# A new issue order and new PSUM banks for an attention and gated feed-forward kernel

## The chip, the cores and the metric

The kernel runs on one core of a Trainium2 chip. Its time is the device time of one launch in microseconds (us); lower is better. Each matmul's inputs are bf16, the tensors in memory are float32.

## The reference

For each of 8 batches and 8 heads (sequence 1024, head size 64) K and V are projected along the sequence to 64 rows, the queries attend to those 64 rows, and the heads are joined to rows of 512. Each of the 8192 rows then goes through a gated layer: 512 to 1536 twice (gate and value), the product of both, and 1536 back to 512.

```python
def _attn_ref(q, k, v, E, F):
    k_proj = np.einsum('ks,bhsd->bhkd', E, k)
    v_proj = np.einsum('ks,bhsd->bhkd', F, v)
    scores = 1.0 / np.sqrt(q.shape[-1]) * np.matmul(q, k_proj.transpose(0, 1, 3, 2))
    scores = scores - np.max(scores, axis=-1, keepdims=True)
    attn = np.exp(scores)
    attn = attn / (np.sum(attn, axis=-1, keepdims=True) + 1e-09)
    return np.matmul(attn, v_proj)

def _moe_ref(x, w_gate, w_val, w_out):
    gate = 1.0 / (1.0 + np.exp(-(x @ w_gate)))
    return gate * (x @ w_val) @ w_out

x = attn_out.transpose(0, 2, 1, 3).reshape(8192, 512)   # between the two
```

## The kernel before

**Stages.** For each batch, K and V (tiles KVs) are loaded by GpSimd's DMA queue in two halves each (KV00 and KV01 for K, KV10 and KV11 for V; 4 heads in each), and Q (tile Qb) in two halves, Q0 and Q1. TensorE projects K and V with E and F (tile EFT) in one job, `kv` (L1494, 16 matmuls). ScalarE keeps the result in kpd, and SyncE turns it with a transposing DMA into kpD (L1523). SyncE also turns Q with four transposing DMAs, qT0 to qT3 (`transpose_q`, L1480); qT0 and qT1 need Q0, qT2 and qT3 need Q1. Scores, exponentials and sums follow, SyncE turns the exponentials (eT, four DMAs), TensorE multiplies them by V, and SyncE turns the joined rows into xT (four DMAs). The gated layer on a block of 512 rows uses sums of blocks of its operands (xS, tG, tV, hS), so that a product of 2 x 2 blocks takes seven block products and not eight (`quad_jobs`, `seven`, `o_jobs`). The output leaves in stores on SyncE's queue, 256 KB each.

Batch p + 2 is loaded, and batch p + 1 attended to, while the rows of batch p go through the gated layer. The first batch is apart: it is loaded in smaller pieces, in step with the weights (wG, wV), and K, Q and the exponentials are turned on TensorE, which at the start waits for loads anyway. There 35 fills, matmuls of an identity that nobody reads (`busy`, L720, 128x256, into a bank of their own), stand between the useful ones.

**Order.** The program is cut into 2902 jobs, each for one engine (some matmuls into one bank, one copy, one DMA issue). ORDER is a written-out list of their numbers, with -1 for a fill, and PLACES names the PSUM bank, or the number of the working buffer, of each of 906 slots. Nothing else decides: `Scheduler.job` takes a time `release` for each job and makes no use of it, and `Scheduler.run` only reads the two lists.

```python
    def job(self, eng, pos, body, release=0.0, name=""):
        self.jobs.append(Job(eng, body, name))
...
        for s, p in zip(slots, PLACES):
            s.at = p
        return [fill if i < 0 else self.jobs[i].body for i in ORDER]
```

Each engine runs its own jobs in the order of the list, and waits by semaphores for what they read, or for readers of what they overwrite; a DMA issue waits in its engine's line like any other instruction. TensorE's fills and SyncE's and GpSimd's DMA issues all stand in this one list.

The times in K_AT, Q_AT, V_AT (L784) and LAND (L1011), when loads are taken to land, are used for `release` alone.

**Names in the profile.** pA and pF are PSUM banks; all matmuls are recorded at L518, ScalarE's copies at L532, GpSimd's DMA issues at L559, the transposing DMAs at L1483 (qT), L1526 (kpD) and L1741 (xT), and the stores at L1302.

Of the kernel before, what the change touches and what calls it, by code (L numbers as in the profile page):

```python
# [153 lines left out]
class Job:  # L154
# [5 lines left out]
    0, -1, -1, -1, 1, 2, -1, -1, -1, -1, -1, -1, 14, 3, -1, 4, 15, 12, 5, -1, 6, 13, -1, 16, 22, 17, -1, 7, 23,  # L160
    18, 19, 8, -1, -1, -1, 24, 34, 9, 20, 25, -1, -1, 10, 32, 35, 11, 21, 33, 26, -1, -1, -1, -1, -1, -1, -1,
    -1, -1, 36, 42, 28, 37, 52, 43, 38, 53, 39, 27, 44, 54, 29, -1, 30, 45, 40, 59, 55, 31, 46, -1, -1, -1, -1,
    -1, 56, 41, 60, 57, 47, 48, 58, 169, 61, -1, -1, 50, 49, 119, 62, 168, 51, 112, 346, 63, 118, 174, 64, 65,
    113, 124, 176, 128, 126, 125, 180, 130, 129, 127, 178, 114, 131, 115, 116, 165, 120, 68, 175, 122, 66, 121,
    69, 67, 123, 86, 88, 179, 87, 76, 70, 89, 136, 71, 177, 77, 144, 72, 140, 181, 78, 73, 90, 79, 74, 96, 167,
    152, 146, 164, 91, 142, 148, 154, 97, 75, 138, 153, 92, 132, 93, 155, 94, 149, 134, 80, 145, 98, 160, 81,
    147, 99, 161, 95, 117, 150, 162, 151, 82, 133, 100, 84, 83, 102, 101, 85, 137, 103, 190, 166, 106, 135, 104,
    108, 183, 141, 163, 107, 139, 105, 301, 187, 192, 109, 185, 302, 143, 198, 110, 214, 111, 199, 182, 278,
    170, 215, 262, 189, 303, 200, 171, 263, 216, 184, 191, 202, 201, 173, 264, 304, 188, 266, 203, 172, 217,
    218, 305, 205, 279, 196, 230, 193, 219, 186, 204, 265, 395, 280, 206, 221, 281, 267, 220, 222, 209, 207,  # L170
    269, 223, 210, 246, 270, 396, 211, 231, 225, 212, 227, 234, 197, 247, 308, 232, 397, 208, 273, 233, 250,
    226, 309, 248, 235, 398, 236, 251, 237, 213, 228, 253, 274, 224, 294, 238, 229, 254, 239, 252, 295, 241,
    249, 296, 243, 307, 255, 240, 282, 297, 257, 244, 242, 259, 256, 306, 537, 298, 258, 283, 299, 245, 260,
    285, 531, 156, 286, 261, 300, 538, 535, 289, 158, 533, 157, 290, 323, 159, 332, 314, 310, 315, 337, 319,
    429, 311, 194, 312, 316, 313, 324, 317, 426, 320, 430, 318, 333, 325, 334, 326, 328, 321, 427, 423, 329,
    322, 428, 338, 335, 327, 330, 339, 331, 268, 431, 195, 424, 341, 336, 347, 271, 354, 340, 284, 355, 351,
    342, 356, 432, 425, 352, 357, 348, 343, 349, 272, 287, 350, 344, 353, 288, 345, 359, 366, 433, 363, 275,
    367, 532, 539, 291, 434, 534, 368, 549, 360, 358, 276, 361, 369, 546, 364, 362, 365, 375, 547, 292, 378,
    370, 376, 371, 536, 548, 550, 372, 377, 277, 551, 379, 373, 293, 380, 383, 390, 374, 552, 391, 384, 385,
    540, 381, 392, 553, 541, 386, 382, 387, 555, 545, 388, 393, 389, 556, 415, 394, 499, 416, 515, 417, 500,  # L180
    418, 435, 516, 501, 436, 503, 542, 502, 519, 517, 504, 439, 520, 518, 437, 440, 522, 557, 505, 438, 400,
    521, 523, 451, 402, 506, 524, 442, 507, 401, 526, 443, 508, 510, 544, 441, 554, 511, 512, 543, 446, 452,
    513, 528, 447, 444, 453, 399, 455, 419, 445, 448, 529, 456, 483, 421, 514, 558, 527, 509, 467, 420, 484,
    454, 559, 422, 530, 458, 468, 487, 449, 403, 459, 489, 560, 488, 471, 404, 525, 462, 564, 472, 490, 463,
    457, 491, 766, 474, 473, 768, 475, 460, 485, 469, 476, 669, 470, 494, 486, 480, 670, 478, 450, 492, 464,
    479, 770, 671, 481, 477, 685, 461, 409, 482, 493, 672, 686, 495, 406, 765, 673, 410, 675, 465, 405, 674,
    496, 769, 689, 411, 676, 466, 690, 412, 771, 497, 677, 687, 413, 678, 733, 407, 688, 692, 414, 682, 498,
    679, 749, 408, 693, 767, 691, 734, 680, 683, 696, 563, 681, 694, 735, 561, 750, 772, 695, 736, 751, 697,
    773, 565, 737, 752, 684, 774, 738, 566, 583, 753, 567, 740, 584, 569, 568, 775, 570, 754, 578, 741, 777,
    585, 780, 779, 571, 744, 574, 579, 781, 572, 575, 586, 756, 573, 745, 698, 580, 782, 592, 576, 587, 701,  # L190
    581, 562, 588, 785, 577, 593, 757, 596, 582, 786, 702, 589, 760, 597, 787, 705, 590, 594, 703, 789, 591,
    598, 704, 601, 761, 595, 790, 599, 602, 699, 605, 608, 603, 707, 600, 606, 706, 609, 717, 700, 604, 610,
    739, 607, 791, 617, 611, 708, 742, 718, 613, 755, 709, 778, 614, 612, 618, 719, 615, 619, 721, 743, 758,
    616, 746, 722, 720, 620, 712, 621, 625, 759, 783, 622, 713, 626, 623, 710, 784, 747, 776, 724, 711, 624,
    762, 788, 627, 629, 748, 637, 628, 714, 630, 638, 796, 725, 631, 641, 792, 639, 715, 728, 640, 642, 763,
    716, 632, 644, 905, 633, 645, 643, 646, 906, 634, 900, 764, 723, 635, 793, 726, 647, 636, 867, 729, 803,
    868, 665, 883, 648, 902, 804, 730, 667, 869, 666, 731, 805, 668, 870, 871, 794, 806, 807, 727, 872, 809,
    797, 808, 795, 819, 732, 798, 874, 907, 899, 810, 875, 908, 904, 811, 901, 878, 652, 812, 873, 879, 814,
    649, 903, 816, 884, 876, 651, 914, 815, 813, 887, 820, 880, 885, 877, 881, 821, 888, 817, 823, 835, 799,
    824, 909, 886, 836, 822, 890, 912, 826, 801, 891, 851, 839, 650, 889, 840, 910, 894, 892, 882, 837, 895,  # L200
    915, 911, 838, 842, 827, 896, 852, 653, 917, 843, 897, 855, 913, 893, 853, 856, 830, 854, 858, 831, 841,
    859, 846, 800, 857, 898, 802, 847, 862, 860, 916, 825, 918, 654, 828, 659, 863, 844, 845, 656, 864, 861,
    660, 1037, 829, 919, 655, 1038, 848, 661, 1039, 849, 920, 663, 1133, 1040, 832, 865, 1053, 921, 657, 1041,
    833, 1054, 923, 1137, 818, 662, 1057, 850, 1135, 1055, 1042, 922, 924, 1058, 658, 834, 1044, 1060, 1134,
    1045, 1056, 926, 664, 866, 1043, 925, 927, 1138, 1061, 1046, 1101, 928, 1059, 1102, 1117, 1062, 932, 1047,
    933, 1050, 931, 934, 929, 1105, 1051, 1103, 1048, 1063, 1104, 1066, 1049, 935, 937, 1064, 1136, 936, 1139,
    1067, 1118, 1140, 1065, 1119, 938, 1141, 1121, 1120, 1106, 946, 1142, 1122, 939, 942, 947, 1124, 940, 1143,
    943, 1052, 941, 1125, 1108, 948, 1145, 1147, 951, 944, 1148, 1109, 952, 955, 1146, 945, 1112, 956, 949,
    1149, 1113, 953, 1144, 950, 960, 1150, 1069, 957, 964, 954, 1153, 961, 930, 1070, 1154, 962, 958, 1071, 965,
    963, 959, 969, 1073, 970, 1155, 966, 1128, 971, 1123, 1068, 967, 1157, 972, 1129, 1072, 968, 973, 1085,  # L210
    1074, 974, 976, 981, 1076, 977, 982, 978, 975, 1158, 1086, 1126, 979, 983, 988, 985, 1087, 1077, 986, 980,
    989, 984, 1130, 987, 990, 993, 1088, 997, 1089, 991, 994, 1107, 998, 1131, 1090, 1075, 992, 995, 1110, 1080,
    1159, 1092, 999, 1111, 1000, 1078, 1114, 1093, 1009, 1001, 1151, 1115, 1081, 1002, 1152, 1010, 1127, 1116,
    1003, 1005, 1011, 1091, 1006, 1012, 1156, 1096, 996, 1007, 1082, 1079, 1097, 1163, 1273, 1008, 1004, 1083,
    1274, 1013, 1033, 1014, 1235, 1132, 1164, 1015, 1160, 1236, 1034, 1171, 1016, 1094, 1237, 1172, 1161, 1238,
    1095, 1187, 1162, 1275, 1173, 1084, 1268, 1239, 1166, 1035, 1098, 1174, 1165, 1272, 1175, 1240, 1270, 1251,
    1267, 1188, 1242, 1176, 1269, 1189, 1243, 1178, 1022, 1099, 1191, 1179, 1282, 1036, 1100, 1192, 1182, 1190,
    1252, 1246, 1019, 1271, 1183, 1194, 1247, 1167, 1020, 1241, 1195, 1255, 1244, 1018, 1193, 1256, 1169, 1198,
    1017, 1253, 1199, 1258, 1177, 1259, 1248, 1180, 1262, 1026, 1254, 1203, 1276, 1196, 1204, 1025, 1184, 1263,
    1181, 1205, 1197, 1257, 1206, 1283, 1249, 1219, 1260, 1284, 1277, 1185, 1220, 1200, 1245, 1278, 1207, 1201,  # L220
# [155 lines left out]
def bass_linformer_attn__then__ffn_glu_sigmoid_kernel(  # L376
# [20 lines left out]
    with contextlib.ExitStack() as es:  # L397
# [383 lines left out]


        def first_batch():
            K_AT, Q_AT = ((6.4, 8.05), (10.65, 12.0)), ((9.35, 13.4), (28.8, 30.1))  # L784
            V_AT = ((15.9, 15.9), (18.35, 19.45))
            ENGS = ("ACT", "DVE", "POOL")

# [1117 lines left out]
```

## Time and profile before

| | |
|---|---|
| time, median of 3 runs | 518.26 us (517.63 to 518.54) |
| the profiled execution | 518.57 us, its span 516.8 us |
| clock of TensorE granted | 1.00 in every slice |
| TensorE busy | 510.5 us, 99% of the span, 4741 matmuls |
| VectorE, ScalarE, GpSimd busy | 436.6, 374.4, 169.8 us |
| moved by DMA | 71.57 MB, 138 GB/s in the mean |
| hardware queue (SyncE's), software queue (GpSimd's) | 40.91 MB in 104560 packets, 29.89 MB in 35904 |

The span is the time from the first to the last instruction of the profiled execution; the launch takes 1.8 us more. The profile models the end of a matmul, so that a busy TensorE may still hold small gaps: from start to start a fill of 256 columns takes 0.109 us, while its row shows 0.274. Shares are of the span, and "x" is a number of instructions. A transposing DMA is issued by SyncE (SPq), and its landing is later than the end of its issue.

### The profile page before, as it was taken

Reading aid. Unit: us, or ns where it says so; the run is one execution under the profiler, and the core shown is the slowest. Engines: PE = TensorE matmul, PEld = TensorE weight load, DVE = VectorE, ACT = ScalarE, POOL = GpSimd, SP = SyncE. Lnnn points to the kernel's source line nnn. Section 1 sums busy time; section 2 is a strip of 40 time slices with the busy share of each in tenths; the row PEclk is TensorE's granted clock in tenths of the full one; section 3 lists DMA queues with packets and bytes.
Section 4 is the critical chain, followed back from the end, with each engine's and each line's share of the span. In section 5 each row is a group of like instructions: output and inputs, shape, how many; then the busy total and the mean of one; then the engine's idle time right before and its main releaser. Section 6 shows DMA issues by size and latency. Waiting matters only on the chain.

```text
span 516.8 us, 12171 instructions
## 1 busy us (share of the span) xinstructions
PE 510.5 (99%) x4741; PEld 426.6 (83%) x4741; DVE 436.6 (84%) x849; ACT 374.4 (72%) x714; POOL 169.8 (33%) x196
## 2 busy tenths in 40 slices
PE   8999999999999999999999999999999999999997
PEld 4555867889988899888998888888998889988884
DVE  6769998699988899869997799978989889968771
ACT  1566956888876796767867789777878679686652
POOL 9882004520435033340245113620053502403020
PEclk9999999999999999999999999999999999999999
DMA  9999938896679946995579957796545994530204
GB/s 159 198 198 207 181 70 175 136 201 124 148 148 170 188 92 128 155 179 115 119 143 174 158 103 128 156 196 113 142 98 129 202 169 104 96 90 1 82 2 162
DMA packets 140521, 71.57 MB, mean 138 GB/s; under 512 B 97200, under 2 KB 132272, under 8 KB 140464
## 3 DMA queue, kind: packets, MB, share of 16 engines
q1 hardware_dynamic: 104560, 40.91, 37.8%
q0 software_dynamic: 35904, 29.89, 37.8%
q8 instruction: 37, 0.61, 0.5%
q14 instruction: 20, 0.16, 0.1%
HBM read 60.29 MB, written 16.78 MB: 149 GB/s over the span
## 4 chain that ended last, share of the span: by engine, by line
PE 55%; DMA 3%; issue 1%; POOL 1%; ACT 0%; POOLq 0%
PE pF L518 28%; PE pA L518 27%; DMA KVs<-in_k_dram 3%; POOL KVs L559 0%; POOL Qb L559 0%; ACT ost L532 0%; POOL xS L547 0%; POOLq L129 0%
## 5 line engine op out<-in xcount | busy, mean ns | idle before, releaser
L532 ACT ACTIVATE spare<-pF 128x512 f32<-128x512 f32 (+2 forms) x167 | 94.2, 574 | 32.0 <-PE pF L518 22.7
L547 POOL TENSOR_TENSOR hT<-hT,hS 128x512 bf16<-128x512 bf16 x42 | 48.1, 1164 | 174.2 <-PE pA L518 96.8
L532 ACT ACTIVATE spare<-pA 128x512 f32<-128x512 f32 (+2 forms) x146 | 83.7, 586 | 20.2 <-PE pA L518 16.3
L1724 POOL TENSOR_TENSOR KVs<-spare,inv 128x384 bf16<-128x384 f32 (+1 forms) x41 | 29.6, 731 | 84.4 <-DVE topf L1635 35.3
L532 ACT ACTIVATE spare<-spare 128x512 f32<-128x512 f32 x74 | 46.1, 628 | 5.9 <-DVE spare L1146 5.5
L1146 DVE TENSOR_TENSOR spare<-pF,spare 128x512 f32<-128x512 f32 x59 | 40.1, 681 | 10.5 <-PE pF L518 5.2
L1215 DVE SCALAR_TENSOR_TENSOR hT<-spare,pF 128x512 bf16<-128x512 f32 x60 | 40.8, 679 | 7.7 <-PE pF L518 3.7
L518 PE MATMUL pA<-wO,hT 128*128 128x256 bf16 (+1 forms) x336 | 47.2, 280 | 0.0
L1146 DVE TENSOR_TENSOR spare<-pA,spare 128x512 f32<-128x512 f32 x54 | 36.7, 681 | 8.8 <-PE pA L518 6.4
L1215 DVE SCALAR_TENSOR_TENSOR hT<-spare,pA 128x512 bf16<-128x512 f32 x52 | 35.3, 678 | 8.3 <-PE pF L518 4.1
L518 PE MATMUL pF<-wO,hT 128*128 128x256 bf16 (+1 forms) x276 | 42.2, 296 | 0.0
L518 PE MATMUL pF<-xT,wV 128*128 128x256 bf16 (+1 forms) x248 | 39.9, 283 | 0.0
L518 PEld LDWEIGHTS pA<-wO,hT 128*128 128x128 bf16 x336 | 32.8, 98 | 6.5 <-ACT KVs L532 0.2
L518 PE MATMUL pA<-xS,wV 128*128 128x256 bf16 x248 | 37.2, 273 | 0.0
L518 PE MATMUL pA<-xT,wG 128*128 128x256 bf16 (+1 forms) x220 | 35.4, 284 | 0.6 <-DVE xT L876 0.5
L518 PE MATMUL pF<-xS,wG 128*128 128x256 bf16 x232 | 34.1, 272 | 0.0
L518 PEld LDWEIGHTS pF<-wO,hT 128*128 128x128 bf16 x276 | 26.6, 98 | 8.7
L518 PE MATMUL pF<-xS,tV 128*128 128x256 bf16 x224 | 33.6, 273 | 0.0
L518 PE MATMUL pA<-xS,tG 128*128 128x256 bf16 x208 | 31.2, 273 | 0.0
L518 PE MATMUL pF<-xT,wG 128*128 128x256 bf16 (+1 forms) x188 | 30.9, 286 | 0.0
L532 ACT ACTIVATE EF<-pA 128x512 f32<-128x512 f32 (+2 forms) x35 | 19.7, 564 | 14.4 <-PE pA L518 13.5
L518 PEld LDWEIGHTS pF<-xT,wV 128*128 128x128 bf16 x248 | 23.9, 98 | 4.3
(186 smaller groups left out, 1288.7 us busy)
## 6 DMA issues: line engine op xcount, KB each, us to landing
out_dram<-ost SPq DMA_DIRECT2D x63, 256.0 KB, 2.4
KVs<-in_v_dram POOLq DMA_DIRECT2D x15, 512.0 KB, 9.4
KVs<-in_k_dram POOLq DMA_DIRECT2D x14, 512.0 KB, 10.2
Qb<-in_q_dram POOLq DMA_DIRECT2D x14, 512.0 KB, 8.8
wO<-in_moe_w_out_dram POOLq DMA_DIRECT2D x1, 1536.0 KB, 28.1
wG<-in_moe_w_gate_dram POOLq DMA_DIRECT2D x5, 256.0 KB, 16.9
wV<-in_moe_w_val_dram POOLq DMA_DIRECT2D x5, 256.0 KB, 17.3
KVs<-in_k_dram POOLq DMA_DIRECT2D x4, 256.0 KB, 6.8
```

Source lines behind the costliest of these rows:

```text
L518: lambda e: e.matmul(o, lhsT, rhs, **kw),
L532: lambda e: e.activation(o, i, func, scale=scale),
L547: fn = lambda e: e.tensor_tensor(o, a, b, op)
L1146: lambda e: e.tensor_tensor(PB(b)[:, :] if stay else BF(s), PB(b)[:, :], BF(s), ALU.add),
L1215: lambda e: e.scalar_tensor_tensor(o, y.rearrange("p (j c) -> p j c", j=2), 1.0, x.rearrange("p (j c) -> p j c", j=2), ALU.add, ALU.mult,),
L1724: fn = lambda e: e.tensor_tensor(xto.rearrange("p (g h d) -> p h g d", g=2, h=H)[:, hh[0] : hh[1], :, :], o[:, :, 0:DH].rearrange("p (h g) ...
```

## The change

ORDER is another permutation of the same 2902 jobs, with 58 fills where there were 35; the 23 more stand, as all the fills, in the first part of the list (the last one is entry 123, it was entry 94). PLACES holds other numbers in its 906 entries. The times of K_AT, Q_AT, V_AT and LAND are new too. So TensorE has 4764 matmuls instead of 4741; all other engines have as many instructions as before, in another order, and the DMAs move the same bytes.

The first 25 loads of GpSimd's queue keep their order. Later the order within each batch's six loads is another one, and so is the order of SyncE's transposes and stores. In batch 4, of which the prediction speaks, jobs 1017 to 1022 are the loads KV00, KV01, KV10, KV11, Q0 and Q1, jobs 1023 to 1026 the transposes qT0 to qT3, and job 1027 is `kv`. The order before was 1022, 1019, 1020, 1018, 1017, 1026, 1025, 1021, 1027, 1024, 1023; it becomes 1018, 1017, 1021, 1022, 1019, 1020, 1025, 1023, 1026, 1027, 1024.

From issue to use, counted in TensorE time along the list, the shortest stretches are 3.6, 4.2 and 4.3 us for kpD in batches 3, 4 and 5 (the shortest was 5.1) and 3.9 us for eT in batches 4 and 5 (it was 4.9).

The diff, cut to its core:

```diff
 ORDER = (
-    0, -1, -1, -1, 1, 2, -1, -1, -1, -1, -1, -1, 14, 3, -1, 4, 15, 12, 5, -1, 6, 13, -1, 16, 22, 17, -1, 7, 23,
-    18, 19, 8, -1, -1, -1, 24, 34, 9, 20, 25, -1, -1, 10, 32, 35, 11, 21, 33, 26, -1, -1, -1, -1, -1, -1, -1,
-    -1, -1, 36, 42, 28, 37, 52, 43, 38, 53, 39, 27, 44, 54, 29, -1, 30, 45, 40, 59, 55, 31, 46, -1, -1, -1, -1,
-    -1, 56, 41, 60, 57, 47, 48, 58, 169, 61, -1, -1, 50, 49, 119, 62, 168, 51, 112, 346, 63, 118, 174, 64, 65,
...
+    0, -1, -1, -1, -1, -1, -1, 1, 2, 3, -1, -1, -1, -1, -1, -1, -1, 14, 12, 15, 4, 13, 5, -1, -1, -1, -1, -1, 6,
+    22, 16, 23, -1, -1, -1, 7, 17, 24, 8, 25, -1, -1, -1, -1, 32, 9, 34, 26, 33, -1, 10, 18, 11, 35, 19, 27, -1,
+    -1, -1, -1, -1, 42, 36, 43, -1, 30, 31, 37, -1, -1, -1, 44, 52, 45, 20, 53, 38, 21, 54, 55, 46, -1, -1, -1,
+    -1, -1, -1, 28, 39, 59, 168, 29, 40, -1, -1, -1, -1, 56, 60, 57, 47, 58, 169, 41, 61, -1, -1, -1, -1, -1,
+    -1, -1, -1, -1, -1, 48, 50, 62, 49, 113, 51, -1, -1, -1, 63, 174, 112, 64, 65, 119, 118, 346, 128, 165, 125,
...
 PLACES = (
-    0, 2, 4, 1, 3, 1, 5, 0, 6, 1, 0, 2, 2, 0, 3, 2, 4, 3, 2, 0, 1, 0, 1, 5, 5, 0, 5, 0, 4, 8, 5, 9, 0, 1, 7, 0,
...
+    0, 3, 4, 2, 2, 1, 6, 1, 5, 0, 2, 0, 0, 1, 4, 3, 3, 2, 1, 2, 1, 1, 2, 0, 0, 1, 7, 0, 1, 7, 7, 9, 5, 7, 0, 7,
...
-            K_AT, Q_AT = ((6.4, 8.05), (10.65, 12.0)), ((9.35, 13.4), (28.8, 30.1))
-            V_AT = ((15.9, 15.9), (18.35, 19.45))
+            K_AT, Q_AT = ((7.05, 8.4), (11.1, 12.45)), ((9.8, 13.75), (29.1, 30.45))
+            V_AT = ((16.35, 16.35), (17.7, 20.3))
...
         LAND = {
-            "G": (20.1, 21.45, 26.1, 34.2, 23.5, 31.5, 36.85),
-            "V": (20.75, 22.15, 27.5, 35.5, 24.8, 32.9, 38.25),
+            "G": (20.5, 21.75, 26.4, 34.65, 23.75, 32.1, 37.3),
+            "V": (21.05, 22.45, 27.8, 36.0, 25.05, 33.35, 38.7),
         }
```

## The prediction

> **What bounds the kernel now.** I read the page first (busy shares, then the chain of waits), then TensorE's waits, the windows of the start, and around the one wait left the chain, SyncE's timeline and the landings of single transfers.
>
> ```profile
> PE 510.5 (99%) x4741; PEld 426.6 (83%) x4741; DVE 436.6 (84%) x849; ACT 374.4 (72%) x714; POOL 169.8 (33%) x196
> PE 55%; DMA 3%; issue 1%; POOL 1%; ACT 0%; POOLq 0%
> PE pF L518 28%; PE pA L518 27%; DMA KVs<-in_k_dram 3%; POOL KVs L559 0%; POOL Qb L559 0%; ACT ost L532 0%; POOL xS L547 0%; POOLq L129 0%
> ```
>
> TensorE is busy for 99% of the span, and the chain holds little but its matmuls and one load of K. An order that does the same matmuls can gain only where TensorE waits. All of its waits (total us, times, longest):
>
> ```profile
> PE pA L518 <- DMA KVs<-in_k_dram: 1.1, 2, 0.9
> PE pA L518 <- DVE tV L642: 1.1, 1, 1.1
> PE pA L518 <- DVE xT L876: 0.5, 1, 0.5
> PE pF L518 <- ACT EFT L532: 0.3, 1, 0.3
> PE pF L518 <- ACT eT L532: 0.2, 1, 0.2
> PE pF L518 <- ACT kpd L532: 0.2, 1, 0.2
> ```
>
> The same list from 50 us on keeps only the 0.9 us on K. Everything else is in the start (window; PE, PEld, DVE, ACT, POOL busy; clock; DMA share; GB/s):
>
> ```profile
> 5.00:10.00 5.00, 4.60 (x38) 3.06 (x37) 2.99 (x10) 0.60 (x1) 5.00 (x8) 1.00 1.36 175
> 10.00:15.00 5.00, 4.57 (x59) 3.15 (x57) 3.64 (x10) 1.49 (x3) 5.00 (x8) 1.00 1.38 201
> 20.00:25.00 5.00, 4.79 (x47) 2.11 (x46) 3.46 (x8) 2.61 (x5) 3.13 (x4) 1.00 1.45 195
> 45.00:50.00 5.00, 4.47 (x50) 3.03 (x48) 5.00 (x13) 3.92 (x9) 0.07 (x1) 1.00 1.24 208
> 50.00:60.00 10.00, 10.00 (x94) 8.70 (x92) 10.00 (x20) 9.10 (x19) 0.00 (x0) 1.00 1.24 207
> ```
>
> Up to 50 us the loads run at about 200 GB/s and TensorE has small holes; some of its work there is fills, which compute nothing:
>
> ```profile
> L518 PE MATMUL pA<-ident 128*128 128x256 bf16 x35 | 5.8, 274 | 0.0
> ```
>
> (274 ns includes a modelled end; from start to start a fill takes 0.109 us, so 35 take 3.8 us.) The late wait, as the chain shows it (start, us):
>
> ```profile
> 212.36 2.25 POOL KVs L559 x3
> 214.61 16.57 DMA KVs<-in_k_dram
> 231.17 0.04 issue
> 231.22 1.99 PE pA L518 x16
> ```
>
> A load of K issued at 214.61 lands 16.57 us later, and the kv projection starts behind it. What held it up is on SyncE's queue:
>
> ```profile
> 216.76 19.77 SPq L1483 DMA_TRANSPOSE qT<-Qb  x3
> 236.62 1.27 SPq L1526 DMA_TRANSPOSE kpD<-kpd  x1
> ```
>
> In batch 4 the load Q1 is issued ahead of the four K/V loads and lands at 216.74; at once qT3 and qT2 transpose it, beside those loads. The loads land at 220.86, 224.85, 227.88 and 231.17, 3.0 to 4.0 us apart; in batch 5, with no transpose beside them, at 278.11, 280.89, 283.41 and 285.90, about 2.6 apart. The transposes suffer more: qT3 takes 14.2 us to land, qT2 16.7 (its issue alone holds SyncE 6.75), where alone one lands 3.0 to 3.3 after its issue.
>
> **The change, part by part.** The times in K_AT, Q_AT, V_AT and LAND only go to `release`, which `Scheduler.job` does not use: cost nothing. PLACES keeps 906 entries: other PSUM banks, no other instructions. ORDER keeps all 2902 jobs and has 58 fills, not 35. So matmuls, copies, DMAs and bytes are as before; what counts is 23 fills, the stalls and where each transfer now stands.
>
> *Fills.* 23 x 0.109 = 2.5 us of TensorE time, all before 23 us. They cost nothing where they fill a wait, and 2.5 us where they don't. Walking the new order with the old landings and step lengths: the first projections start when K lands (8.41, 11.10, 12.43) and Q (9.78), each some 0.1 to 0.2 us later than before, because fills now end after the landing. The scores of the first tile come 0.3 earlier, the first product with V (job 56) starts at 20.49 in both, behind V (20.31) and a copy. Up to 29 us the new order falls 0.4 to 0.9 us behind in useful work; there both wait for Q (29.09, 30.41), and both turn Q11 at 30.45. The new order owes two plain gate and value products then (0.86 us), but meets the weights wG2 and the copy into xT later, where before lost 0.24 and 0.69 us. At 49.4 us both have done the same jobs: the start is worth 0, give or take 0.4.
>
> *The wait at 231 us.* In the new batch 4, KV01 and KV00 come first, then Q0 and Q1, then KV10 and KV11. That step was 1.05 us longer than the matmuls need (0.9 as a wait): -1.05. The kpD transpose of batch 7, which started 0.15 us late behind a qT, has room now: -0.15, and some 0.1 of small waits.
>
> *New collisions.* With Q0 and Q1 in the middle, qT2, qT0, qT3 and two stores are issued on top of KV10 and KV11. By the old cadences (2.6 undisturbed, up to 4.0 with transposes) KV11 lands 19.4 to 23 us after the batch's first issue; kv stands 21.3 after it. Between no stall and 1.7 I take 0.45, as the middle, 21.2, just meets kv. In batch 3 KV11 is due 18.4 to 19.3 after the first issue and wanted at 19.8: 0 to 0.5, I take 0.05. The other batches have 1.5 us or more to spare.
>
> *Shorter distances.* From issue to use the new order leaves 3.6 us to kpD in batch 3 (least before: 5.1), 4.2 and 4.3 in batches 4 and 5, and 3.9 to two eT transposes (before: 4.9). kpD took 2.8 to 3.9 us undisturbed and 5.0 to 5.2 beside other transfers, eT mostly 3.1, four of 24 over 3.75. So 0 to 1.5 us for kpD, of which I take 0.15, near the undisturbed end, since the batch's loads have landed by then, and 0.05 for eT. The Trainium skill ("Advanced Engine Details and Errata", X-Bar Transpose) says that transposes on this chip are as fast as regular DMAs. By that they would land like the stores, 2.4 us, and this term would be nothing; this trace agrees only loosely where nothing else moves (3.0 to 3.3) and not at all beside loads.
>
> *Sum.* -1.05 - 0.15 - 0.1 + 0.45 + 0.05 + 0.15 + 0.05 + 0 = -0.6. The profiled run took 518.57 us (span 516.8 and 1.8 around it): 517.97. It lies 0.31 over the median of the three runs, 518.26: 517.7.
>
> **The rivals.**
>
> *Clean gain.* All distances hold and the start is equal or up to 0.4 better: -1.3, down to -1.7, so 517.0 (516.6). For it: none of before's chains over ACT and DVE, at the same least distances, stalled after 50 us. Against: batch 4's margin is nil by the middle of the estimate.
>
> *Batch 4 collides again, slower.* Three qT transposes and two stores meet KV10 and KV11, as two met four loads before. If each load takes 4.0 us and not 2.6 and the third transpose holds SyncE some 6.75 us as qT2 did, KV11 lands 1.7 late (what waits for qT and kpD behind it is pushed back as far). With 1.0 for kpD and 0.1 for eT, and the removed 1.3, that is 1.7 + 1.0 + 0.1 - 1.3 = +1.5: 519.8 by the profiled run's 520.07. It decides as soon as KV11 lands over 22.6 us after the batch's first issue. The Trainium skill ("DMA: Bandwidth & Descriptors", Queues, rings and completion order) speaks for it: each DMA engine goes round-robin between queues, packet by packet. Transposes have many small packets (6744 packets for 2.35 MB on the hardware queue from 205 to 240 us, against 3168 for 3.15 MB on the software queue), and the slower cadence there agrees with shared turns.
>
> *Fills not covered, slower.* If the start's loads land as in before but the extra fills delay each of its short chains, half or all of the 2.5 us stays: 519.2 to 520.8. Against: both orders meet again at Q11's landing.
>
> *The change does not do what it says.* The landings spread no more than before and a new stall takes the old one's place: 518.3.
>
> **How the numbers follow.** A measurement of this kernel tells some 0.2% (1.04 us) from no change. Forecast, 0.38: of which 0.10 ends beyond -1.04. Clean gain, 0.27: 0.25 beyond, 0.02 within. Batch 4 collides, 0.22: 0.20 slower, 0.02 within. Fills, 0.07, slower. Nothing, 0.06, within. That makes faster 0.35, within 0.28 + 0.02 + 0.02 + 0.06 = 0.38, slower 0.27. The range goes from the clean gain's best (516.6) to the collision (519.8): what is left out is some of the fills and a worse collision, under 0.2. The likeliest case alone spans 517.1 to 518.8.
>
> **What would show it.** Right: TensorE's waits from 50 us on hold no KV of 0.9 us, and at the step to kv in batch 4 nothing over 0.5; about 50 us the new trace does the same matmuls within 0.4 us of the old. Wrong: a wait of 1 us or more on KV, qT or kpD between 150 and 300 us (collision); Q11 turned later than 30.6 us, or the plain products at 50 us behind by over 0.5 (fills); waits on eT or kpD of several tenths in each batch (distances).

## The result, and the profile after

The changed kernel takes 522.0 us in the median (four runs, 521.82 to 524.24), the kernel before beside it 518.05: a ratio of 1.0087, 95% interval 1.0067 to 1.0106. (The medians alone give 1.0076; the run of 524.24 us has an ordinary span, 520.1, and 4.1 us around it.) That is slower by over four times the 0.2% that a measurement can tell, where no change or a small gain was forecast. A second comparison of the same two kernels gave 1.0089 (1.0072 to 1.0105). The profiled execution took 521.82 us with a span of 519.6: 2.8 us more in the span, and 2.2 us around it where before had 1.8.

The same first lines of the page, busy shares and chain:

```profile
PE 513.2 (99%) x4761; PEld 428.0 (82%) x4764; DVE 441.2 (85%) x849; ACT 374.0 (72%) x714; POOL 170.3 (33%) x196
...
PE 94%; DVE 2%; DMA 2%; ACT 1%; issue 0%
```

TensorE has 2.7 us more of busy time, about the 2.5 us of the 23 fills. That says nothing of whether they fill waits; the load of K has left the chain, and VectorE, ScalarE and a transpose of eT have come in. TensorE's waits from 50 us on (total us, times, longest):

```profile
PE pA L519 <- DVE hT L548: 1.1, 1, 1.1
PE pF L519 <- DMA eT<-KVs: 0.4, 1, 0.4
PE pF L519 <- ACT KVs L533: 0.3, 1, 0.3
```

One wait of 0.9 has gone, three others have come, none of them on the loads that the prediction looked at. Around batch 4's kv the chain now holds TensorE alone (start, us; before, the load of K stood here):

```profile
231.84 0.44 PE pA L519 x4
232.27 1.89 PE pF L519 x16
```

To see all of the loss, and not only what the list of waits names, I summed for every execution the shortest step, over all profiled runs, from each matmul to the next one, and compared how much of this work two executions had done at the same time. The table gives what each run lost (+) or won on the kernel before in each stretch, in us; the edits of the lower rows are told below. (A wait in these sums is from start to start: the 1.1 us in the list above is 1.25 here.)

| run | up to 54 | 66 to 90 | 90 to 230 | 230 to 235 | 235 to 340 | 340 to 350 | 430 to 450 | all, at 510 |
|---|---|---|---|---|---|---|---|---|
| changed kernel | +0.42 | +0.84 | +0.54 | -0.98 | +0.38 | +1.25 | +0.58 | +2.84 |
| changed, again | +0.22 | +1.12 | +0.52 | -0.97 | +0.38 | +1.26 | +1.07 | +3.38 |
| after_fills35 | -0.14 | +0.60 | +1.47 | -0.97 | +0.37 | +1.25 | +0.10 | +2.49 |
| after_sum3 | +0.09 | +0.59 | +0.64 | -0.98 | +0.37 | -0.01 | +1.01 | +1.55 |
| after_pool | 0.00 | +0.58 | +0.90 | -0.97 | +0.38 | 0.00 | +0.88 | +1.60 |
| after_fix4 | +0.05 | +0.72 | +1.16 | -0.98 | +0.38 | 0.00 | +0.23 | +1.39 |
| after_fix6 | +1.21 | +1.20 | +0.53 | -0.99 | +0.38 | +0.01 | +0.07 | +2.18 |
| before_fills58 | +0.99 | 0.0 | 0.0 | -1.02 | 0.0 | 0.0 | 0.0 | -0.20 |
| before_q1 | +0.27 | 0.0 | 0.0 | -1.03 | 0.0 | 0.0 | 0.0 | -0.95 |
| before_q1k | -0.11 | 0.0 | 0.0 | -1.02 | 0.0 | 0.0 | 0.0 | -1.32 |

(The stretches that are left out hold under 0.2 each. 0.0 stands for less than 0.05.) The gain that was forecast at 231 us is there to a tenth. What was not forecast is four other places: 66 to 90, 340 to 350, 430 to 450, and small waits in between.

*340 to 350 us.* The chain of the changed kernel:

```profile
341.87 0.69 DVE spare L1147
342.56 2.49 DVE hT L548
345.05 0.05 issue
```

A sum of two 128x512 bf16 tensors on VectorE (job 2008, half of sum3), whose 13 sisters take 0.41 to 1.29 us, took 2.57, and TensorE's product (2023) stood for 1.25 us. GpSimd's timeline at that time:

```profile
341.11 1.15 POOL L548 TENSOR_TENSOR hT<-hT,hS 128x512 bf16<-128x512 bf16 x1 [5.19 <-PE pA L519]
342.23 0.79 POOL L560 DMA_DIRECT2D KVs<-in_k_dram  x1
343.04 1.17 POOL L548 TENSOR_TENSOR hT<-hT,hS 128x512 bf16<-128x512 bf16 x1
344.14 1.53 POOL L560 DMA_DIRECT2D Qb<-in_q_dram  x2
```

The new order puts the load KV00 of batch 6 between two of GpSimd's sums, and VectorE's sum starts (342.47) inside that load's issue. It ends at 345.04, 0.12 us after the issue of the next load.

*430 to 450 us.* The chain, and the DMA queues from 440 to 448 us (packets, MB, share):

```profile
442.35 4.56 DMA eT<-KVs
446.91 0.05 issue
446.96 0.35 PE pF L519 x3
```

```profile
q8 instruction: 1, 0.02, 0.9%
```

The transpose eT3 landed 4.56 us after its issue, not 3.1. One packet of 16 KB on an instruction queue ran from 444.89 to 446.09 on one of the DMA engines, just when eT3 would have landed (445.4). The same in batch 1: eT3 issued at 83.49, such a packet from 86.57 to 87.67, landed at 88.66. Two packets of 8 KB on the other instruction queue (q14, some 20 packets in a run) stand beside that one too, at 85.27 and 86.56. There are 37 packets of 16 KB in a run, one to about 128 matmuls. Of the transposes with no load beside them, in the eleven profiles of the table and of before, those without a 16 KB packet (counted from 0.9 us after their issue) land 3.14 to 3.21 us after their issue in the median of a run, those with one 3.8 to 4.5, and up to 5.6. In what follows a fetch is such a packet.

### The profile page after: what moved, and what is told of

Same layout as the page of the kernel before. It is cut to its first block, busy times and chain, and to the rows that moved or that the text cites. A ratio compares the mean times of both kernels' runs of the same rounds, so it can differ in the third digit from the quotient of the medians.

```text
span 519.6 us, 12214 instructions
## 1 busy us (share of the span) xinstructions
PE 513.2 (99%) x4761; PEld 428.0 (82%) x4764; DVE 441.2 (85%) x849; ACT 374.0 (72%) x714; POOL 170.3 (33%) x196
## 4 chain that ended last, share of the span: by engine, by line
PE 94%; DVE 2%; DMA 2%; ACT 1%; issue 0%
PE pA L519 49%; PE pF L519 45%; DMA eT<-KVs 2%; DVE hT L548 1%; DVE hT L1216 1%; DVE hS L548 0%; DVE topf L1636 0%; ACT KVs L533 0%; ACT ost L533 0%; DVE spare L1147 0%; DVE pF L1147 0%; DVE pF L1663 0%; ACT EFT L533 0%; ACT EF L533 0%; DVE hT L1057 0%
## 5 line engine op out<-in xcount | busy, mean ns | idle before, releaser
L533 ACT ACTIVATE spare<-pA 128x512 f32<-128x512 f32 (+2 forms) x161 | 92.9, 585 | 35.3 <-PE pA L519 26.9
L533 ACT ACTIVATE spare<-pF 128x512 f32<-128x512 f32 (+2 forms) x151 | 84.2, 566 | 29.6 <-PE pF L519 18.7
L1725 POOL TENSOR_TENSOR KVs<-spare,inv 128x256 bf16<-128x256 f32 (+1 forms) x45 | 32.1, 723 | 80.9 <-DVE topf L1636 35.8
L533 ACT ACTIVATE spare<-spare 128x512 f32<-128x512 f32 x80 | 49.6, 628 | 5.5 <-DVE spare L1147 5.1
L519 PE MATMUL pF<-wO,hT 128*128 128x256 bf16 (+1 forms) x251 | 38.6, 298 | 0.4 <-ACT KVs L533 0.3
L519 PE MATMUL pF<-xS,wV 128*128 128x256 bf16 x240 | 35.7, 273 | 0.0
L519 PE MATMUL pF<-xT,wV 128*128 128x256 bf16 (+1 forms) x216 | 35.3, 286 | 0.0
L548 POOL TENSOR_TENSOR xS<-xT,xS 128x512 bf16<-128x512 bf16 x14 | 16.9, 1210 | 51.1 <-DVE xS L548 36.2
L519 PE MATMUL pA<-xT,wV 128*128 128x256 bf16 (+1 forms) x192 | 31.1, 284 | 0.0
L519 PE MATMUL pA<-xS,wG 128*128 128x256 bf16 x192 | 28.1, 273 | 0.0
```

What stands on the lines that cost most here:

```text
L519: lambda e: e.matmul(o, lhsT, rhs, **kw),
L533: lambda e: e.activation(o, i, func, scale=scale),
L548: fn = lambda e: e.tensor_tensor(o, a, b, op)
L1725: fn = lambda e: e.tensor_tensor(xto.rearrange("p (g h d) -> p h g d", g=2, h=H)[:, hh[0] : hh[1], :, :], o[:, :, 0:DH].rearrange("p (h g) ...
```

## The experiments

Each run stands beside the kernel before, which read 517.78 to 518.96 us in the median of these comparisons; differences from the changed kernel cross two of them, so the table, made from single profiles, is the finer measure of where time went.

**before_q1**, the forecast's own term by itself: the order before, where job 1022 (Q1 of batch 4) goes behind the four K and V loads.

```diff
-1022, 1019, 1020, 1018, 1017, 1026, 1025, 1021, 1027
+1019, 1020, 1018, 1017, 1022, 1026, 1025, 1021, 1027
```

Expected: 

> The order before, with one job moved: in batch 4 the load Q1 is issued behind the four K and V loads instead of ahead of them. If the wait of 0.9 us at 231 us came from the two qT transposes that ran beside those loads, the loads land about 2.6 us apart, kv starts at about 230.2 us and the kernel is 1.0 us faster than before. If the loads were late for another reason, kv waits as before: no change.

Measured: 517.54 us, the kernel before 518.45 beside it: 0.9979 (0.9963 to 0.9995). The loads landed at 216.98, 219.97, 222.45 and 225.45, 3.0, 2.5 and 3.0 us apart, and TensorE did not wait (chain: start, us):

```profile
230.14 0.44 PE pF L487 x4
230.58 1.85 PE pA L487 x16
```

So the place of Q1 was the cause of the wait, and it was worth 1.0 us. The move takes away two things at once, the transposes beside the loads and the 512 KB of Q1 ahead of them. Here five loads in a row, without transposes, took 16.7 us from the first issue (211.32) to the last landing (227.99), where Q1 and the four took 20.7 in the kernel before. By that the loads would have landed at about 227.1 behind Q1 alone, 3 us early; so the transposes were needed for the wait. But the turn of Q1, some 2.5 us, is also more than the 0.9 that was waited, and no run took one away without the other.

**after_fills35**: 23 fills out of the changed order, its 13 groups of them cut to 3, 6, 2, 1, 2, 1, 4, 0, 2, 4, 2, 5 and 3.

Expected: 

> The changed order with 23 fills taken out, so that 35 are left, spread as the 58 were. Theory A (the loss is a sum of stalls behind 50 us, fills lie in waits): at most 0.4 us from the start. It also moves the 16 KB instruction fetches (about one per 125 matmuls) some 23 matmuls later against the work, so that the eT3 transposes of batches 1 and 7 no longer meet one: they land 3.1 us after their issue and not 5.2 and 4.6, and the waits of 0.24 and 0.52 us are gone. Together 0.6 to 1.2 us faster than the changed kernel, still 2.5 or more slower than before. Rival B (the 23 fills are the loss): 2.5 us faster than the changed kernel.

Measured: 521.54 us (1.0052, 1.0032 to 1.0072, beside a slower reading of the kernel before); its span, 519.2, is 0.4 under the changed kernel's. Rival B is out: the start gained 0.56 us and not 2.5. Both eT3 waits are gone (430 to 450: +0.10). In batch 7 eT3 met no fetch and landed in 3.12 us, as foretold; in batch 1 it met none of 16 KB but again the two of 8 KB, and still took 4.37, not 3.1: enough for its stretch of 5.0, but the 16 KB packets are not all of its lateness there. But eT1 of batch 3, issued at 192.51, now met one and landed 4.62 us later, and TensorE waited 0.61 for it; another 0.36 came up at 180 us on a sum of VectorE (plusG), behind work of VectorE without a gap. The phase of the fetches chooses which transpose is hit. The long sum repeated to the hundredth:

```profile
342.61 2.57 DVE L516 TENSOR_TENSOR hT<-hT 128x512 bf16<-128x512 bf16 x1
```

**after_sum3**: job 2008 one place earlier on VectorE.

```diff
-1993, 2014, 1927, 1996, 1941, 1928, 2008, 1943
+1993, 2014, 1927, 2008, 1996, 1941, 1928, 1943
```

Expected: 

> The changed order with one VectorE job moved: the second half of sum3 of a block (job 2008) one place earlier, ahead of job 1996, where VectorE was idle for 1.3 us. If the wait of 1.1 us at 345 us is this job's late and long (2.57 us) run, that wait is gone and the kernel is 1.2 us faster than the changed one. If the long run is only a sign of something else, the wait stays or moves: within 0.3 us of the changed one.

Measured: 520.94 us (1.0043, 1.0029 to 1.0058), 1.1 under the changed kernel, its span 1.3 under. The wait is gone. The next sum of two tensors on VectorE (an xs) now stands in the old place, begins at 342.00 beside the same load and sum, and takes 2.58 us itself; nobody waits for it. So it is the place beside GpSimd's work that is slow, and not the job.

**after_pool**: VectorE's order left alone, GpSimd's changed.

```diff
-2014, ..., 1754, ..., 2016, ..., 1757, 1758, 2015   (GpSimd: sum, load, sum, loads, sum)
+2014, ..., 2016, 1754, ..., 1757, 1758, 2015        (GpSimd: sum, sum, load, loads, sum)
```

Expected: 

> The changed order with one GpSimd job moved: the load KV00 of batch 6 (job 1754) behind the next sum (2016), so that GpSimd does sum, sum, load, load, load and not sum, load, sum, load, load beside VectorE's job 2008. VectorE's order is the changed one. If GpSimd's instructions hold VectorE's sum of two SBUF tensors, it now waits for one sum only and takes about 1.2 us in place of 2.57; TensorE's wait of 1.1 us at 345 us goes, 1.2 us faster than the changed kernel. If VectorE's job is long for a reason of its own, it still takes 2.5 us and the time is the same.

Measured: 520.38 us (1.0044, 1.0027 to 1.0062); the wait is gone, and job 2008 took what was expected:

```profile
342.18 1.18 DVE L517 TENSOR_TENSOR hT<-hT 128x512 bf16<-128x512 bf16 x1
```

With two runs from two sides, the cause of the 1.25 us is shown: VectorE's sum was held beside GpSimd's load KV00 of batch 6, in a place where a product of TensorE needed it at once. Which of GpSimd's instructions holds it is not shown. The next sum on VectorE (an xs) took over the long run here, as in after_sum3, though no sum of GpSimd ran beside it, only load issues:

```profile
343.28 1.43 DVE L517 TENSOR_TENSOR xS<-xT 128x512 bf16<-128x512 bf16 x1
```

```profile
340.81 2.26 POOL L517 TENSOR_TENSOR hT<-hT,hS 128x512 bf16<-128x512 bf16 x2 [5.13 <-PE pA L488]
343.03 0.79 POOL L529 DMA_DIRECT2D KVs<-in_k_dram  x1
343.80 1.50 POOL L529 DMA_DIRECT2D Qb<-in_q_dram  x2
```

And in the changed kernel itself the same row of GpSimd's instructions, sum, load (of Q, at 157.70), sum, held nothing: VectorE's sum that starts in that issue, 0.26 us behind its start, took 0.42 us.

```profile
157.96 0.42 DVE L548 TENSOR_TENSOR hS<-hS,hT 128x512 bf16<-128x512 bf16 x1
```

**after_fix4**: after_sum3, and 312 ahead of 533 on VectorE, 552 behind 551 and 2607 ahead of 2481 on TensorE.

Expected: 

> The changed order with its four largest stalls behind 50 us removed by moving single jobs: sum3 (2008) ahead of 1996; the tile's subtraction 312 ahead of the sum 533 on VectorE; and a half product (552, 2607) put ahead of the attention product that waits for eT3 in batches 1 and 7. If the loss is the sum of these stalls: 1.25 + 0.51 + 0.24 + 0.52 = 2.5 us faster than the changed kernel, so within 1.5 us of before. If stalls return elsewhere once these are gone: under 1.5 us faster.

Measured: 520.09 us (1.0030, 1.0017 to 1.0043), 1.9 under the changed kernel where 2.5 was expected. The waits on job 429 (0.51) and on eT3 of batch 1 are gone, that on eT3 of batch 7 fell to 0.20 (it took 4.89 us this time, and the half product covers 0.65). But 0.35 and 0.31 came back at 79 and 80 us, on the weight sums 194 and 195 of VectorE: in the table 66 to 90 costs 0.72, hardly less than before the edit. And 0.58 came at 180.7 us, where after_fills35 had 0.36, again behind VectorE (90 to 230: +1.16).

**after_fix5** and **after_fix6** put these sums earlier and both halves (2607, 2608) ahead of 2481. In after_fix5 one edit was wrong, as the expectation of after_fix6 says; its time (521.36, 1.0065, 1.0048 to 1.0082) holds that edit's wait, 1.42 us at 72 us.

Expected of after_fix5: 

> As after_fix4, with two more edits: both half products (2607, 2608) ahead of the attention product that waits for eT3 in batch 7, and on VectorE the tile's maximum 311 ahead of 290 and the weight sums 194 and 195 ahead of the subtraction 330, since in after_fix4 the wait of 0.5 us at 73 us came back as 0.35 and 0.31 on these sums. If the waits can be taken away one by one, 0.8 us faster than after_fix4 (519.3). If VectorE bounds the stretch from 70 to 90 us, the wait comes back a third time: at most 0.3 faster than after_fix4.

Expected of after_fix6: 

> after_fix5 put the tile's maximum 311 ahead of the scores 310 that it reads (it took the maximum of old data, and TensorE's next write of that bank waited for it), so its 1.3 us wait at 72 us is the edit's own. Here 311 stays behind 310, and the job 290 is put behind it; the other edits are the same. If the waits can be taken away one by one, the waits of after_fix4 at 79 and 80 us (0.35, 0.31) and on eT3 in batch 7 (0.20) go: a span of about 517.3 us, 0.8 faster than after_fix4. If VectorE bounds the stretch from 70 to 90 us, they come back: 517.9 or more.

after_fix6: 520.63 us (1.0035, 1.0022 to 1.0047), a span of 518.9, of which 1.21 us were lost in the start; so the stretches decide and not the span. The wait on eT3 in batch 7 is gone though eT3 took 4.86 us. From 66 to 90 us the loss came back a third time, 0.75 on an exponential of ScalarE and 0.39 on the copy leaveO, behind VectorE's subtractions: 1.20 in all. In the changed kernel VectorE is busy for 19.53 of the 20 us from 70 to 90; in the kernel before it is for 10.00 and 7.62 of the two halves. That VectorE bounds the stretch agrees with this, and with three edits that moved the wait and did not remove it; an order that frees it was not found, so it is argued more than shown.

**before_fills58**: 23 more fills in the order before (groups of 5, 10, 2, 2, 2, 2, 5, 3, 14, 2, 8 and 3).

Expected: 

> The order before with 23 more fills, spread as its 35 are. Fills' own cost: the order before waits some 1.5 us of its first 30 us at places with fills, so of 2.5 us some 0.8 to 1.6 remain. All instruction fetches now come 23 matmuls earlier against the work. Theory A (a transpose that meets a fetch lands up to 5.6 us after its issue; only the shorter distances of the changed order let that reach TensorE): behind 60 us no wait on eT over 0.3 us. Rival (the phase of the fetches alone makes the loss): waits of 0.5 us on transposes in this order too. Rival B (fills are never covered): 2.5 us slower than before.

Measured: 518.72 us against 518.32: 1.0009 (0.9996 to 1.0023). The start lost 0.99, as expected, and no transpose was waited for behind 60 us, though 17 of those without a load beside them met a fetch, up to 5.20 us. So in this phase the fetches do no harm at the longer distances of the order before. It is one draw: that order's shortest stretch for eT is 4.9 us, and landings of 5.2 and 5.4 us occur. The 0.99 came back at 231 us: TensorE arrived 1.0 us later at a load of K that landed at 231.14 (before: 231.17), so the wait was used up. Here the late start was free, since a later wait stood at a fixed time.

**before_best** was to be before_q1 with two more jobs moved.

Expected: 

> before_q1 with two more jobs moved: on VectorE the copy into xT (job 111) ahead of a weight sum and a gate (185, 143), and on SyncE the kpD transpose of batch 7 (2134) ahead of qT2 (2129). If the waits of 0.69 us at 49 us and 0.15 at 426 go: up to 0.8 us faster than before_q1, 1.8 than before. If VectorE bounds the stretch up to 50 us, the 0.69 comes back on the next sums: 0.2 faster than before_q1.

Measured: 523.47 us (1.0102, 1.0087 to 1.0118). The second move put the transpose ahead of the half copy that it reads (batch 7's kpD takes that half from the batch before), so the copy, and ScalarE's queue behind it, waited for the transpose: 4.1 us on TensorE, and behind it the granted clock of TensorE was 0.67 from 425 to 430 us (1.00 around it). It says nothing of the question. The first move is readable: the wait of 0.69 at 49 us went, and 0.70 came at 50.87 on VectorE's next sum. That fits VectorE as the bound there.

**before_q1k** puts the second move right.

Expected: 

> before_q1 with the transpose qT2 of batch 7 (2129) put behind kpD (2134). In before_best kpD was put ahead of the second half of the copy that it reads, and the copy then waited for the transpose, which made that run's 4.1 us. Here the copy stays ahead. The wait of 0.15 us at 426 us goes: 0.15 faster than before_q1, 1.1 us faster than before. If qT2, now later, is waited for: the same as before_q1 or slower.

Measured: 517.53 us, the kernel before 518.96: 0.9974 (0.9964 to 0.9983). The wait at 426 us is gone (span 515.5), but by the times it can't be told from before_q1. It is the best order found, 4.5 us under the changed kernel, and one moved job of the old order makes nearly all of it.

**after_again**: the changed kernel unedited.

Expected: 

> The changed kernel once more, unedited, beside the kernel before. What the order fixes should repeat: VectorE's sum of 2.57 us and TensorE's wait of 1.25 us at 345 us, 0.5 at 73 us. What instruction fetches and landings decide should vary: the waits on eT3 in batches 1 and 7 between 0.2 and 1.0 each, the start between 0 and 1.2 us behind the order before. Span 519.6 to 520.5, time 3.3 to 4.3 us over the kernel before, of it 0.4 outside the span.

Measured: 522.21 us against 517.78. The sum took 2.57 us, the waits of 1.25 and 0.51 repeated to the hundredth. The waits on eT3 were 0.51 and 1.00 (0.24 and 0.52 in the first profile), with landings 5.44 and 5.05 us after the issue.

## Why the prediction was wrong

*Right.* The wait at 231 us was priced at -1.05 and gave -0.98; before_q1 shows that Q1's place made it, though not the transposes apart from Q1's turn. kpD of batch 7 gave its 0.15. The start was put at 0, give or take 0.4: five profiles of this start with 58 fills lie 0.0 to 0.42 behind the kernel before, and two, where the first K loads landed late (8.73 and 9.22 us against 7.8 to 8.2), 0.9 and 1.2. Fills as the loss (a rival at 0.07) are refuted by after_fills35. (The lower end of that rival, 519.2, does not come out of its own terms: half of 2.5 us over 518.26 is 519.5.)

*Wrong without harm.* In batch 4 the new collision took 0 of 0.45: KV11 landed 19.6 us after the first issue, at the early end of 19.4 to 23, and 1.8 before kv. The transposes did meet KV10 and KV11, as the rival said, but landed in 3.9 to 6.3 us, and the two loads came 2.6 and 2.9 us behind the landing before them: a load beside transposes is not always as slow as the 4.0 of the kernel before. kpD of batch 3 was no trouble either (3.1 us, used 4.4 after its issue).

*The step that failed first* is the term for eT. It was sized at 0.05 us from "eT mostly 3.1, four of 24 over 3.75", and cost 0.9 in one profile and 1.7 in another (stretches 66 to 90 and 430 to 450 together, less 0.5 for job 429). The count does not come out of the trace of before either: of its 28 eT three are over 3.75 (3.81, 4.30, 4.33), and its six kpD landed in 3.1 to 3.5 us, not 2.8 to 5.2. The trace had the warning: eT1 4.33 and xT0 4.80 with no load beside them. I took them for scatter. They were a second population, with an instruction packet in their way, which a list of the packets beside the late landings would have shown. I also looked for it in batches 4 and 5, where the stretches were shortest; it came in batches 1 (a stretch of 5.0 us, no shorter than the least of before, 4.9) and 7 (4.1). In before the same two transposes were missed by the 16 KB packets: eT3 of batch 7 landed 3.1 us after its issue, 2.7 before its use, and eT3 of batch 1, beside two packets of 8 KB, in 3.81.

*The step that failed most* is one with no term at all. The prediction priced the chains over ScalarE and VectorE at nothing, since their least distances were those of before ("none of before's chains ... stalled after 50 us"). Equal distances are not equal waits: what an engine does beside the chain decides. Job 2008 lost 1.25 beside GpSimd, job 429 lost 0.51 to a sum ahead of its subtraction, and single copies of ScalarE came 0.1 to 0.2 late (0.12 at 122, 0.14 at 176 and 0.14 at 305 us, which come again in all runs of this order, the last with up to 0.19). With the stretches in which these lie (0.54 and 0.38, of which more than half is traced to no wait) that is 2.7 us, and the removed 1.0 stands against it.

*Outside the span* lie 0.4 us. All orders made from the changed one have 2.2 us or more around the span, all made from before 1.7 to 1.9. The changed ones fetch 8 KB of instructions 1.0 to 1.3 us behind the span's end (at 520.86 us in the first profile); in those from before the last such fetch is at 493 to 499 us. That the late fetch makes the 0.4 is the likely reading, but no run took it away.

The times add up so: 2.84 in the span and 0.4 around it make 3.25, the difference of the two profiled executions. The medians differ by 3.95; the first profile of the changed kernel is the fastest of its runs (spans 519.6 to 520.1), and that of the kernel before, 518.57, lies above all four of its runs in this comparison (517.63 to 518.54).

## What to carry to other kernels

In a kernel whose first engine is 99% busy, a new order has one known wait to win and every short stretch to lose: price each stretch by the slowest landing of its kind in the trace, not by the common one, and ask of each late landing what else moved then. Count what stands beside a chain on every engine, not only its length. And take the one known wait by moving the one job that makes it: that gave 0.2% here, where a whole new order gave it too and lost four times as much elsewhere.

## What the runs showed of the hardware

VectorE's sums of two 128x512 tensors in SBUF wait for GpSimd's sums: beside one of them a sum of 0.41 us takes up to 1.38 and ends 0.28 us after GpSimd's. The Trainium skill ("SBUF — State Buffer", SBUF: two separate sides) calls the port pair that both use an exclusive lock, held for a whole instruction; that agrees with these. It does not give the 2.57 us, in which the sum started during a GpSimd load issue, outlasted the next GpSimd sum by 0.84 us, and ended 0.12 after the following issue. Load issues alone mostly hold nothing (0.41 or 0.42 us beside issues in all sixteen cases of the first traces of the two kernels), but after_pool has one that does: 1.43 us, ending 0.15 after the issue of the next load. In all eight profiles of the changed order and its edits the long run falls on the sum that starts 0.24 to 0.26 us into the issue of the same load, KV00 of batch 6, and ends 0.12 to 0.15 us after the issue of the next one. Why that issue and not the others stays open.

Instruction packets of 16 KB last 0.9 to 2.6 us each, counted as the time of one DMA engine (1.2 us are 0.9% of 16 engines over 8 us). A transpose that meets one lands 0.7 to 1.3 us later in the median than one that meets none, and up to 2.4. That it then waits for a last part on the engine that the packet holds is the likely reading; the profile does not name engines. That the packets are TensorE's instructions is inferred from their number (one per 128 matmuls) and from their shift with the fills: with 23 more fills in the order before, the packet at 444.43 us comes at 441.94, and 23 fills take 2.5 us.
